# Whole-row gathers through DRAM in place of quarter-row gathers, in a routed mixture-of-experts kernel

## The chip, the cores and the metric

One core of a Trainium2 chip. The metric is device time in microseconds (us) for one execution of the whole program; lower is better. Five engines run their own instruction streams and meet at semaphores: TensorE (PE, matmul), VectorE (DVE), ScalarE (ACT), GpSimd (POOL) and SyncE (SP, which here only issues transfers). POOL issues the indirect DMAs (transfers whose row numbers come from a table in SBUF); SP issues the plain ones.

## The reference

A linear-attention layer `a` and a mixture-of-experts layer `b` read the same 2,048 tokens of 448 channels; a sigmoid gate mixes them. The expert part is what the change touches:

```
logits = xf @ w_gate                          # 8 experts
topk_idx = argsort(-logits)[:, :2]            # two experts for each token
gates = softmax(topk_val)
for e in range(8):
    h = silu(xf @ w1[e]) @ w2[e]              # 448 -> 1792 -> 448
    out = out + gate_of_e * h
out = g * a + (1 - g) * out
```

## The kernel before, in words

The first 230 us or so compute the attention layer and route the tokens. Routing writes, for each token and expert, a record (token number, weight) into a table in DRAM; the table is read back so that `idm` holds, for each expert, 4 columns of 128 token numbers, and `idx` the numbers of tokens over 512. Experts are handled in order of load: the code's expert 0 is the fullest. The room of an expert is fixed: 552, 544, 544, 504, 504, 504, 496 and 488 tokens (`ROOMS`, L31), so experts 0, 1 and 2 have a fifth, small chunk of 40, 32 and 32 tokens. The diff counts experts from 0; "experts 2 to 8" in the change's name are the code's 1 to 7.

An expert is 14 steps (`fc`, L1145), one for each 128 of its 1,792 hidden channels. A step has these parts:

- `load` (L726, transfers at L721): SP loads the weights of a pair of steps, 512 KB of `w1` and 448 KB of `w2`, into `wr` buffers. It is called one pair ahead of `halve`; the `w1` buffer exists twice, the `w2` buffer five times.
- `halve` (L733): ACT copies the weights into TensorE's float32r format, which keeps the high part (L739, `w1h`, `w2h`), and DVE subtracts to get the rest (L741, `w1l`, `w2l`). It is called for the pair after the current one.
- `first` (L943): TensorE computes `hp` for all tokens of the expert with 11 matmuls (L115), in one bank of PSUM for 504 tokens or fewer and in two halves for experts 0 to 2. There are two such banks. ACT applies silu (L961, `hs`), DVE makes the high and low parts `hx` (L967, L970).
- `second` (L988): one or two steps later TensorE multiplies `hx` by `w2` and adds into four or five PSUM accumulators `acc` (L1021, and L1004 for the small chunk).

At the end of an expert `leave` (L1032) scales the accumulators (L1038, L1040) and POOL adds the rows into the output in DRAM with indirect DMAs (L934).

The tokens of the next expert are brought in beside these steps. `gather` (L760) is called for chunk `c` at step 4 + `c`, `tokens` (L803) at step 9 + `c`. A token's row in DRAM is 512 floats: four quarters of 128. For expert 0 one indirect DMA fetches 128 whole rows (L768), a token in each partition. For the others the layout is another: partition 32a + i of a chunk holds, for b = 0 to 3, quarter a of token 32b + i. DVE's 32x32 transposes (L816) then give the layout with channels in partitions; ACT and DVE split it into the high and low parts `xgh` and `xgl` (L799, L800) that `first` multiplies. To fetch straight into that layout, four indirect DMAs, one for each b, fetch 128 quarter rows each (L772). Their indices `idq` are made by `quarters` (L921) in the first four steps of expert 0.

The `xg` buffers number five, so a chunk's gather waits until the chunk five before it is used up. The orders of PE, ACT and DVE are written out by hand. Those of POOL and SP are placed by a scheduler from the dependencies and a simulated time; each of the two queues runs its instructions strictly in the order so found.

Of the kernel before, what the change touches and what calls it, by code (L numbers as in the profile page):

```python
# [8 lines left out]
F32 = mybir.dt.float32  # L9
F32R = mybir.dt.float32r  # L10
BF16 = mybir.dt.bfloat16
I32 = mybir.dt.int32
AF = mybir.ActivationFunctionType
ALU = mybir.AluOpType
# [4 lines left out]
P = 128  # L19
# [5 lines left out]
E = 8  # L25
# [7 lines left out]
EX = EXS[0]  # L33
LARGE = len(EXS)
# [16 lines left out]
QASKS = {t: t + 7 for t in range(9)}  # L51
PEND = 0
ROWS = 1
SPLIT = 13
STORES = {3: 4, 4: 4, 5: 4, 6: 4}
VAHEAD = 6
# [18 lines left out]
def gated_mix(ctx: ExitStack, tc: tile.TileContext, xt, xq, wk, wq, wv, wphi, wo, w12, out):  # L75
    nc = tc.nc
    nm = MAIN // P

    cst = ctx.enter_context(tc.tile_pool(name="cst", bufs=1))
    dram = ctx.enter_context(tc.tile_pool(name="dram", bufs=1, space=DRAM))  # L80
# [8 lines left out]
    def after(i, others):  # L89
        for o in others:  # L90
            tc.add_manual_dep(i.ins, o.ins.name, mybir.DependencyInfo(mybir.DependencyClass.Sync,
                                                                      mybir.DependencyReason.DATA),
                              reason="what no_dep between its peers leaves out")

    def follow(i, o):
        tc.add_manual_dep(i.ins, o.ins.name, mybir.DependencyInfo(mybir.DependencyClass.NoSync,
                                                                  mybir.DependencyReason.SCHED_ONLY),
                          reason="what is needed sooner goes first")


    runs = {"on": False, "before": [], "last": [], "kind": None}

    def in_turn(i, kind=None):
        if runs["on"]:
            if kind is None or kind != runs["kind"]:
                runs.update(before=runs["last"], last=[], kind=kind)
            for o in runs["before"]:
                follow(i, o)
            runs["last"].append(i)
        return i  # L110

    def mm3(o, pairs):
        n = len(pairs)
        for i, (a, b) in enumerate(pairs):
            nc.tensor.matmul(o, a, b, start=i == 0, stop=i == n - 1)  # L115

    def split(hi, lo, src, hi_engine="act"):
        if hi_engine == "act":
# [31 lines left out]
    pe = pe_stack.enter_context(tc.tile_pool(name="pe", bufs=1, side="right"))  # L150
# [28 lines left out]
    start = ExitStack()  # L179
# [44 lines left out]
    tabx = cst.tile([P, LARGE, 2], F32, name="tabx")  # L224
    idm = cst.tile([P, E * nm], I32, name="idm")
    idx = cst.tile([EX, LARGE], I32, name="idx")
    idq = cst.tile([P, E, 4 * nm + 2], I32, name="idq")
    nc.gpsimd.memset(idq, 0)
    byrank = cst.tile([P, E], I32, name="byrank")
    nov_i = cst.tile([P, 1], I32, name="nov_i")  # L230
    etile = cst.tile([P, MAXOV], I32, name="etile")
# [7 lines left out]
    m = NSLOT // P  # L239
# [83 lines left out]
    for k, c in enumerate(FIRST):  # L323
# [4 lines left out]
        if k == 0:  # L328
            for i in range(2):
                nc.tensor.matmul(bank("A", f"warm{WARM + i}"), zero.bitcast(BF16)[:, 0:P], zero.bitcast(BF16)[:, 0:512],  # L330
                                 start=True, stop=True)
# [267 lines left out]
    routes = []  # L599
# [27 lines left out]
    def blocks(kvs):  # L627
        nc.scalar.activation(kvs[:, :, 0:56], kvp[:, 0:224].rearrange("p (g f) -> p g f", g=4), AF.Copy)
        yield
        kvt = bank("O", "kvt")  # L630
        for g in range(0, 4, 2):
            nc.tensor.transpose(kvt[:, g * 64:g * 64 + P], kvs[:, g:g + 2].rearrange("p g f -> p (g f)"), ident)
        kv = kvt[:, 0:256].rearrange("p (j d) -> p j d", j=NJ)[:, :, 0:DH + 1]
        nc.scalar.activation(B[:, :, 0:DH + 1], kv, AF.Copy, scale=hsign[:, 0:1])
        nc.vector.tensor_scalar(B[:, :, DH + 1:58], kv, hsign[:, 1:2], None, op0=ALU.mult)
# [4 lines left out]
    for t in range(NT):  # L640
# [17 lines left out]
        if 1 <= t < 5:  # L658
            fold("q", t - 1)
            c = t - 1  # L660
# [43 lines left out]
    b = blocks(kvs)  # L704
# [21 lines left out]
    def load(s):  # L726
        e, q = divmod(s, F // 256)
        if q == 0:
            whose[e] = nc.values_load(byrank[0:1, e:e + 1], engines=SPONLY, min_val=0, max_val=E - 1)
        raws[s] = stage(pm, whose[e], q, f"_{s}", 5)  # L730
# [12 lines left out]
    xg = {}  # L743
    x_rows = xq.rearrange("(s a) k -> s (a k)", a=4)

    def extra(e):
        return EXS[e] if e < LARGE else 0
# [9 lines left out]
        return 4 if narrow(e) else 2  # L757


    def gather(e, c):  # L760
        if c == nm and not extra(e):
            return
        n = 4 if c < nm else -(-extra(e) // 32)
        t = pm.tile([P, 4, P], F32, tag="xg", name=f"xg{e}{c}", bufs=nm + 1)
        xg[e, c] = t
        if e == 0:
            ids, m = (idm[:, e * nm + c:e * nm + c + 1], P) if c < nm else (idx[:, e:e + 1], EX)
            in_turn(nc.gpsimd.indirect_dma_start(out=t[0:m].rearrange("p a k -> p (a k)"), out_offset=None, in_=x_rows,  # L768
                                                 in_offset=bass.IndirectOffsetOnAxis(ap=ids, axis=0)))
            return  # L770
        for b in range(n):
            i = nc.gpsimd.indirect_dma_start(  # L772
                out=t[:, b], out_offset=None, in_=xq,
                in_offset=bass.IndirectOffsetOnAxis(ap=idq[:, e, 4 * c + b:4 * c + b + 1], axis=0))
            if e == 1:
                for o in runs["last"]:
                    follow(i, o)


    def low_parts(pool, t, name, eng=nc.vector):  # L780
        m, n = t.shape[0:2]
# [132 lines left out]
    def rows(lo, hi):  # L914
        in_turn(nc.gpsimd.tensor_scalar(idm[:, lo * nm:hi * nm], tabm.bitcast(I32)[:, lo * nm:hi * nm, 0], float(S - 1), None,
                                op0=ALU.min))
        if lo < LARGE:
            hi = min(hi, LARGE)
            in_turn(nc.gpsimd.tensor_scalar(idx[:, lo:hi], tabx.bitcast(I32)[0:EX, lo:hi, 0], float(S - 1), None, op0=ALU.min))

    def quarters():  # L921
        for a in range(4):
            qs = slice(32 * a, 32 * a + 32)
            for b in range(4):
                nc.vector.tensor_scalar(idq[qs, :, b:4 * nm:4],
                                        idm[32 * b:32 * b + 32].rearrange("p (e c) -> p e c", e=E),
                                        4.0, float(a), op0=ALU.mult, op1=ALU.add)
            nc.vector.tensor_scalar(idq[qs, 0:LARGE, 4 * nm], idx[0:32], 4.0, float(a), op0=ALU.mult, op1=ALU.add)
            nc.vector.tensor_scalar(idq[32 * a:32 * a + EX - 32, 0:LARGE, 4 * nm + 1], idx[32:EX],
                                    4.0, float(a), op0=ALU.mult, op1=ALU.add)  # L930
            yield

    def scatter_add(y, idx_ap):
        return nc.gpsimd.indirect_dma_start(  # L934
# [38 lines left out]
    def pieces(e):  # L973
        return 2 if extra(e) else 1
# [81 lines left out]
    def order(e):  # L1056
        return (*([nm] if extra(e) else []), *range(nm))
# [8 lines left out]
    def part_way():  # L1066
        for g in list(coming):
            if next(g, 0) == 0:
                coming.remove(g)

    at, k = None, 0
    for t in range(NT + 2):
# [28 lines left out]
        if t == PEND:  # L1101
            pe_stack.close()
            pm = ctx.enter_context(tc.tile_pool(name="pm", bufs=2, side="right", reuse_waits="tile"))
# [3 lines left out]
        if at is None and not routes:  # L1107
            routes.append(ranks())
            at = NT
        if at == NT and not stores and not routes:  # L1110
            table()
            at = t
        k = t - (NT if at is None else at)
        if k == ROWS:
            rows(0, 1)
        if k == ROWS + 3:
            rows(1, E)
        if ROWS <= k < ROWS + 3:
            for c in range(2 * (k - ROWS), min(2 * (k - ROWS) + 2, nm + 1)):
                gather(0, c)  # L1120
# [3 lines left out]
        part_way()  # L1124
        if ROWS + 2 <= k < ROWS + 3 + nm:
            g = first_tokens(k - ROWS - 2)
            next(g)
            coming.append(g)
        if SPLIT <= t < SPLIT + 3 and splits:
            if next(splits[0], 0) == 0:  # L1130
# [10 lines left out]
    pf = pf_stack.enter_context(tc.tile_pool(name="pf", bufs=2, reuse_waits="tile"))  # L1141
    load(1)
    held = []
    routes += [quarters(), overflow()]
    for s in range(E * NFC):  # L1145
        e, fc = divmod(s, NFC)
        k, i = divmod(s, 2)
        token = tokens(e + 1, fc - 9) if e + 1 < E and 9 <= fc <= 9 + nm else iter(())
        next(token, 0)
        if i == 0 and k + 2 < E * NFC // 2:  # L1150
            load(k + 2)
        if k + 1 < E * NFC // 2:
            for _ in halve(k + 1, 1 + i):
                pass
        next(token, 0)
        if e + 1 < E and 4 <= fc <= 4 + nm:
            gather(e + 1, fc - 4)
        for hf in range(pieces(e)):
            if (e, fc, hf) not in fill:
                first(e, fc, hf)  # L1160
        held.append((e, fc))
        advance(1)
        if e == E - 1 and fc > NFC - LATE:
            continue

        keep = 1 if e == 0 or fc == 0 or fc >= 7 else 2
        while len(held) > keep:
            h = held.pop(0)
            second(*h)
            if h[1] == NFC - 1:  # L1170
                leave(h[0], order(h[0]))
                if h[0] == E - 2:
                    settle()
# [11 lines left out]
    with tc.tile_pool(name="po", bufs=1) as po:  # L1185
        with tc.For_i(0, n_ov, 1) as it:
# [7 lines left out]
            ids = po.tile([P, 1], I32, name="ov_ids")  # L1194
# [5 lines left out]
                                         in_offset=bass.IndirectOffsetOnAxis(ap=ids[:, 0:1], axis=0))  # L1200
            both(xgh, xgl, by_pe(po, xo, P, "ov"))
            acc = bank("O", "ov_acc")
            for fc in range(NFC):
                q, i = divmod(fc, 2)
# [71 lines left out]
```

## Time and profile before

| | us |
|---|---|
| median of 3 runs (lowest, highest) | 833.13 (832.22, 835.84) |
| the profiled execution | 834.39 |
| its span, first to last instruction | 832.7 |
| PE busy / weight load (PEld) busy | 804.8 / 712.7 |
| DVE busy | 480.2 |
| ACT busy | 317.3 |
| POOL busy | 342.4 |

The profile is one execution. A row of the timeline has the start, the duration, the engine, the line of the kernel, the operation, and in brackets how long the engine had been idle and what ended that. A row of the waits has the engine and what it waited to start, then what it waited for, with the total in us, the number of times and the longest. A row of the windows has the start and end of a stretch, its length, then the busy time (and instructions) of PE, PEld, DVE, ACT and POOL, the clock that TensorE was granted (1.00 is full speed), the busy share of the DMA engines and GB/s.

### The profile page before, as it was taken

What the parts mean: (1) busy time and instruction counts of PE and PEld (TensorE: products, weight loads), DVE (VectorE), ACT (ScalarE), POOL (GpSimd) and SP (SyncE); (2) the same over time, 40 slices, a digit from 0 to 9 for tenths busy, and PEclk for the clock granted to TensorE, in tenths of its full rate; (3) what the DMA queues carried; (4) which work ended last, traced back from release to release, by engine and by line L of the source; (5) the groups of instructions that cost most, each with busy time, mean ns of one, the idle gap of its engine ahead of it and who ended that gap; (6) DMA issues with size and microseconds to landing.
All of it is one profiled execution on the core that took longest, in us unless ns stands there. A gap on an engine that the chain in (4) does not pass through costs nothing. (4 is left out here: it accounts for less than half of the span.)

```text
span 832.7 us, 14729 instructions
## 1 busy us (share of the span) xinstructions
PE 804.8 (97%) x5672; PEld 712.7 (86%) x5672; DVE 480.2 (58%) x1048; ACT 317.3 (38%) x553; POOL 342.4 (41%) x344
## 2 busy tenths in 40 slices
PE   9999999899999899999999999999989999999996
PEld 6988887778999789998999888888878888888885
DVE  4597976456775567456645554654555465375431
ACT  5543454345642334333333342342433334244221
POOL 6666876665406256026614350730531143003003
PEclk9999998999999899999999999999999999999999
DMA  8420000015143226423733362463345237225303
GB/s 231 134 81 2 1 3 24 24 39 172 56 164 136 67 88 170 129 73 125 168 90 122 117 148 98 140 148 107 112 125 133 99 125 185 95 94 134 101 1 44
DMA packets 38910, 85.45 MB, mean 103 GB/s; under 512 B 11216, under 2 KB 19552, under 8 KB 38836
## 3 DMA queue, kind: packets, MB, share of 16 engines
q1 hardware_dynamic: 28612, 67.85, 24.6%
q0 software_dynamic: 10224, 16.61, 10.3%
q8 instruction: 46, 0.75, 0.4%
q14 instruction: 28, 0.23, 0.1%
HBM read 71.62 MB, written 12.82 MB: 101 GB/s over the span
## 5 line engine op out<-in xcount | busy, mean ns | idle before, releaser
L1021 PE MATMUL acc<-w2h,hx 128*128 128x448 f32 (+3 forms) x910 | 278.5, 367 | 3.2 <-DVE hx L967 3.1
L772 POOL DMA_INDIRECT xg<-in_xq_dram,idq x114 | 120.6, 1058 | 224.5 <-ACT xgh L799 172.0
L115 PE MATMUL hp<-xgh,w1h 128*128 128x272 f32 (+4 forms) x616 | 198.0, 336 | 5.7 <-ACT hs L961 3.1
L961 ACT ACTIVATE hs<-hp 128x272 f32<-128x272 f32 (+4 forms) x154 | 74.1, 484 | 323.7 <-issue 204.1
L115 PE MATMUL hp<-xgh,w1l 128*128 128x272 f32 (+4 forms) x616 | 196.9, 335 | 0.0
L1021 PEld LDWEIGHTS acc<-w2h,hx 128*128 128x128 f32 (+3 forms) x910 | 169.2, 186 | 26.3 <-issue 5.3
L967 DVE CAST hx<-hs 128x504 fp32r<-128x504 f32 (+5 forms) x154 | 56.2, 365 | 222.9 <-ACT hs L961 194.6
L1021 PE MATMUL acc<-w2l,hx 128*128 128x448 f32 (+1 forms) x462 | 169.4, 367 | 0.0
L115 PEld LDWEIGHTS hp<-xgh,w1h 128*128 128x128 f32 x616 | 116.3, 189 | 17.2 <-ACT hs L961 3.7
L115 PEld LDWEIGHTS hp<-xgh,w1l 128*128 128x128 f32 x616 | 116.4, 189 | 9.7
L934 POOL DMA_INDIRECT out_dram<-y,tabm x32 | 53.5, 1670 | 160.0 <-ACT y L1038 98.3
L115 PE MATMUL hp<-xgl,w1h 128*128 128x272 f32 (+4 forms) x462 | 104.4, 334 | 0.7 <-issue 0.7
L1021 PEld LDWEIGHTS acc<-w2l,hx 128*128 128x128 f32 (+1 forms) x462 | 85.9, 186 | 8.5
L970 DVE TENSOR_TENSOR hx<-hs,hx 128x276 fp32r<-128x276 f32 (+5 forms) x168 | 85.1, 514 | 5.3
L115 PEld LDWEIGHTS hp<-xgl,w1h 128*128 128x128 f32 x462 | 77.0, 189 | 8.8 <-issue 0.7
L741 DVE TENSOR_TENSOR w1l<-wr,w1h 128x1024 fp32r<-128x1024 f32 x56 | 68.0, 1215 | 3.6 <-ACT w1h L739 2.6
L741 DVE TENSOR_TENSOR w2l<-wr,w2h 128x896 fp32r<-128x896 f32 x56 | 60.3, 1076 | 11.0 <-ACT w2h L739 7.7
L739 ACT ACTIVATE w1h<-wr 128x1024 fp32r<-128x1024 f32 x56 | 58.9, 1052 | 0.0
L739 ACT ACTIVATE w2h<-wr 128x896 fp32r<-128x896 f32 x56 | 52.9, 945 | 0.0
L799 ACT ACTIVATE xgh<-xgt 128x512 fp32r<-128x512 f32 (+5 forms) x35 | 20.9, 597 | 38.1 <-DVE xgt L816 28.8
L586 POOL TENSOR_TENSOR ek<-ek,sk 128x896 f32<-128x896 f32 x16 | 27.1, 1699 | 19.0 <-DVE sk L585 9.1
L455 POOL DMA_INDIRECT tabd<-rec,slot_i x32 | 31.5, 984 | 7.6 <-issue 7.3
(221 smaller groups left out, 1020.8 us busy)
## 6 DMA issues: line engine op xcount, KB each, us to landing
wr<-in_w_dram SPq DMA_DIRECT2D x56, 512.0 KB
wr<-in_w_dram SPq DMA_DIRECT2D x56, 448.0 KB
xr<-in_xt_dram SPq DMA_DIRECT2D x15, 256.0 KB
out_dram<-aos SPq DMA_DIRECT2D x16, 224.0 KB
xg<-in_xq_dram,idq POOLq DMA_INDIRECT x114
out_dram<-zero SPq DMA_DIRECT2D x5, 224.0 KB
wraw_v<-in_wv_dram SPq DMA_DIRECT2D x4, 229.0 KB
wraw_k<-in_wk_dram SPq DMA_DIRECT2D x4, 224.0 KB
```

The costliest lines, as they stand in the source:

```text
L115: nc.tensor.matmul(o, a, b, start=i == 0, stop=i == n - 1)
L455: i = in_turn(nc.gpsimd.indirect_dma_start(out=tabd[:, :], out_offset=bass.IndirectOffsetOnAxis(ap=at, axis=0), in_=what, in_offset=None), ...
L586: in_turn(nc.gpsimd.tensor_tensor(out=by_head(e), in0=by_head(e), in1=s_.unsqueeze(2).to_broadcast([P, 2 * H, DH]), op=ALU.mult))
L739: nc.scalar.activation(h, raws[s][layer - 1], AF.Copy)
L741: nc.vector.tensor_tensor(out=l, in0=raws[s][layer - 1], in1=h.bitcast(F32), op=ALU.subtract)
L772: i = nc.gpsimd.indirect_dma_start(out=t[:, b], out_offset=None, in_=xq, in_offset=bass.IndirectOffsetOnAxis(ap=idq[:, e, 4 * c + b:4 * c ...
L799: nc.scalar.activation(xh, src, AF.Copy)
L934: return nc.gpsimd.indirect_dma_start(out=out, out_offset=bass.IndirectOffsetOnAxis(ap=idx_ap, axis=0), in_=y, in_offset=None, compute_op= ...
L961: nc.scalar.activation(hs[:, tsl], hp[:, 0:n], AF.Silu)
L967: nc.vector.tensor_copy(h[:, tsl], hs[:, tsl])
L970: nc.vector.tensor_tensor(out=h[:, a + o:b + o], in0=hs[:, a:b], in1=h[:, a:b].bitcast(F32), op=ALU.subtract)
L1021: nc.tensor.matmul(acc[e][c][:m, 0:D], l, r, start=fc == 0 and k == 0, stop=fc == NFC - 1 and k == len(pr) - 1)
```

## The change

For experts 1 to 7 an indirect DMA now fetches 128 whole rows into a new tile `rows` (two buffers), a token in each partition; SP writes the tile to a piece of DRAM (`spare`) and reads it back with four plain DMAs, one for each quarter of the row, into the layout that `tokens` wants. The gather of chunk `c` is called at step 2 + `c`, the write at 3 + `c`, the read at 5 + `c`; `tokens` stays at 9 + `c`. The gather also waits for the last matmul that `mm3` has issued up to that point, which is the last `first` of the step before. The index table `idq`, its memset and `quarters` go.

```diff
+ASKED = 2
+FETCHED = 5
...
+    reached = {}
+
     def mm3(o, pairs):
         n = len(pairs)
         for i, (a, b) in enumerate(pairs):
-            nc.tensor.matmul(o, a, b, start=i == 0, stop=i == n - 1)
+            reached["pe"] = nc.tensor.matmul(o, a, b, start=i == 0, stop=i == n - 1)
...
-    idq = cst.tile([P, E, 4 * nm + 2], I32, name="idq")
-    nc.gpsimd.memset(idq, 0)
...
+    rows_of, spare = {}, {}
+
     def gather(e, c):
-        if c == nm and not extra(e):
+        ids, m = (idm[:, e * nm + c:e * nm + c + 1], P) if c < nm else (idx[0:extra(e), e:e + 1], extra(e))
+        at = bass.IndirectOffsetOnAxis(ap=ids, axis=0)
+        if e:
+            rows_of[e, c] = pm.tile([P, 512], F32, tag="rows", name=f"rows{e}{c}", bufs=2)
+            i = nc.gpsimd.indirect_dma_start(out=rows_of[e, c][0:m], out_offset=None, in_=x_rows, in_offset=at)
+            after(i, [reached["pe"]])
             return
+        t = pm.tile([P, 4, P], F32, tag="xg", name=f"xg{e}{c}", bufs=nm + 1)
+        xg[e, c] = t
+        in_turn(nc.gpsimd.indirect_dma_start(out=t[0:m].rearrange("p a k -> p (a k)"), out_offset=None, in_=x_rows,
+                                             in_offset=at))
+
+    def spill(e, c):
+        m = P if c < nm else extra(e)
+        spare[e, c] = dram.tile([m, 512], F32, name=f"spare{e}{c}")
+        nc.sync.dma_start(spare[e, c], rows_of[e, c][0:m])
+
+    def fetch(e, c):
         n = 4 if c < nm else -(-extra(e) // 32)
         t = pm.tile([P, 4, P], F32, tag="xg", name=f"xg{e}{c}", bufs=nm + 1)
         xg[e, c] = t
...
-        for b in range(n):
-            i = nc.gpsimd.indirect_dma_start(
-                out=t[:, b], out_offset=None, in_=xq,
-                in_offset=bass.IndirectOffsetOnAxis(ap=idq[:, e, 4 * c + b:4 * c + b + 1], axis=0))
-            if e == 1:
-                for o in runs["last"]:
-                    follow(i, o)
-
+        for a in range(4):
+            nc.sync.dma_start(t[32 * a:32 * a + 32, 0:n],
+                              spare[e, c][:, a * P:(a + 1) * P].rearrange("(b i) k -> i b k", i=32))
...
-    def quarters():
...
-    routes += [quarters(), overflow()]
+    routes.append(overflow())
...
-        if e + 1 < E and 4 <= fc <= 4 + nm:
-            gather(e + 1, fc - 4)
+        for c in range(nm + (extra(e + 1) > 0) if e + 1 < E else 0):
+            if fc == ASKED + c:
+                gather(e + 1, c)
+            if fc == ASKED + c + 1:
+                spill(e + 1, c)
+            if fc == FETCHED + c:
+                fetch(e + 1, c)
```

More of the change, by code (lines that the diff above doesn't have):

```diff
@@ L765, in gather @@
         xg[e, c] = t
[L766 to L770, printed above, removed]
-        for b in range(n):
-            i = nc.gpsimd.indirect_dma_start(
-                out=t[:, b], out_offset=None, in_=xq,
-                in_offset=bass.IndirectOffsetOnAxis(ap=idq[:, e, 4 * c + b:4 * c + b + 1], axis=0))
-            if e == 1:
-                for o in runs["last"]:
-                    follow(i, o)
+        for a in range(4):
+            nc.sync.dma_start(t[32 * a:32 * a + 32, 0:n],
+                              spare[e, c][:, a * P:(a + 1) * P].rearrange("(b i) k -> i b k", i=32))
     def low_parts(pool, t, name, eng=nc.vector):
@@ L919, in rows @@
             in_turn(nc.gpsimd.tensor_scalar(idx[:, lo:hi], tabx.bitcast(I32)[0:EX, lo:hi, 0], float(S - 1), None, op0=ALU.min))
-    def quarters():
[L922 to L931, printed above, removed]
     def scatter_add(y, idx_ap):
```

## The prediction

> **What bounds the kernel now.** I read the page first, then the expert stage by windows (the first expert from 230 us to about 310, the next two 80 us each, the following ones 70 to 75), then what TensorE waited for after 230 us.
>
> ```profile
> span 832.7 us, 14729 instructions
> ...
> PE 804.8 (97%) x5672; PEld 712.7 (86%) x5672; DVE 480.2 (58%) x1048; ACT 317.3 (38%) x553; POOL 342.4 (41%) x344
> ...
> L772 POOL DMA_INDIRECT xg<-in_xq_dram,idq x114 | 120.6, 1058 | 224.5 <-ACT xgh L799 172.0 <-issue 29.9 <-DVE idq L925 21.1
> ```
> ```profile
> 230.00:310.00 80.00, 75.70 (x463) 71.60 (x463) 48.66 (x151) 26.20 (x50) 31.65 (x31) 0.96 0.33 113
> 310.00:390.00 80.00, 78.95 (x516) 73.33 (x515) 49.26 (x129) 29.99 (x60) 30.34 (x26) 1.00 0.42 120
> 390.00:470.00 80.00, 78.95 (x526) 73.11 (x525) 46.23 (x115) 28.09 (x54) 36.64 (x30) 1.00 0.45 126
> 470.00:545.00 75.00, 75.00 (x356) 64.75 (x356) 40.84 (x74) 26.51 (x40) 31.25 (x25) 1.00 0.43 123
> 545.00:620.00 75.00, 71.83 (x333) 61.74 (x332) 38.67 (x70) 25.99 (x40) 23.12 (x20) 1.00 0.43 128
> 620.00:690.00 70.00, 70.00 (x327) 60.72 (x327) 38.46 (x70) 25.27 (x39) 19.07 (x17) 1.00 0.43 127
> 690.00:765.00 75.00, 75.00 (x353) 65.52 (x352) 42.05 (x76) 29.36 (x44) 11.92 (x8) 1.00 0.41 111
> ```
> ```profile
> PE hp L115 <- issue: 3.3, 2, 2.7
> PE acc L1021 <- DVE hx L967: 3.1, 1, 3.1
> PE hp L115 <- ACT hs L961: 3.1, 3, 1.0
> ```
>
> TensorE is the bound, and the matmuls of the expert stage are not touched. So the change can win only what TensorE loses: 4.30 us of idle time in the first window, 1.05 in each of the next two, 3.17 in the fifth, none in the others: 9.57 us together. The waits agree (9.5 us) and show that it is six gaps. The 114 gathers of POOL cost nothing by their 120.6 us. The question is whether they make the six gaps, so I looked at the two long ones in the timeline.
>
> ```profile
> 271.04 0.54 PE L115 MATMUL hp<-xgl,w1h 128*128 128x276 f32 x3
> ...
> 273.03 0.94 POOL L772 DMA_INDIRECT xg<-in_xq_dram,idq  x1 [0.30 <-issue]
> 273.81 0.40 ACT L961 ACTIVATE hs<-hp 128x276 f32<-128x276 f32 x1 [4.58 <-remote]
> ...
> 274.26 0.60 PE L115 MATMUL hp<-xgh,w1h 128*128 128x276 f32 x1 [2.68 <-issue]
> ...
> 277.35 0.62 PE L115 MATMUL hp<-xgl,w1h 128*128 128x276 f32 x2 [0.66 <-issue]
> ```
> ```profile
> 608.88 0.84 PE L115 MATMUL hp<-xgl,w1h 128*128 128x504 f32 x3
> 609.23 0.94 POOL L772 DMA_INDIRECT xg<-in_xq_dram,idq  x1 [0.30 <-issue]
> 611.76 0.59 ACT L961 ACTIVATE hs<-hp 128x504 f32<-128x504 f32 x1 [6.61 <-remote]
> ...
> 612.86 0.47 PE L1021 MATMUL acc<-w2h,hx 128*128 128x448 f32 x1 [3.13 <-DVE hx L967]
> ...
> 622.48 0.84 PE L115 MATMUL hp<-xgl,w1h 128*128 128x504 f32 x3
> ...
> 623.41 0.59 ACT L961 ACTIVATE hs<-hp 128x504 f32<-128x504 f32 x1 [0.36 <-PE hp L115]
> ```
>
> The reader is to see the delay between a finished `hp` and silu on it. At 623 us `hp` ends at 623.32 and ACT starts at 623.41, 0.09 us later, although POOL is adding output rows then. In the gaps `hp` ends at 271.58 and ACT starts at 273.81, 2.2 us later with nothing else to do; and 609.72 against 611.76, 2.0 us. TensorE then has no free `hp` bank (first gap) or no `hx` (second). Both times POOL is in, or has just ended, a run of quarter gathers one 0.30 us behind the other. The short gaps look the same, for instance:
>
> ```profile
> 303.54 0.40 ACT L961 ACTIVATE hs<-hp 128x276 f32<-128x276 f32 x1 [3.11 <-remote]
> 306.88 0.39 PE L115 MATMUL hp<-xgh,w1h 128*128 128x276 f32 x1 [0.96 <-ACT hs L961]
> ```
> ```profile
> ACT hs L961 <- remote: 27.4, 6, 6.6
> ```
> ```profile
> 675.37 0.95 POOL L772 DMA_INDIRECT xg<-in_xq_dram,idq  x1 [0.31 <-issue]
> 676.12 0.59 ACT L961 ACTIVATE hs<-hp 128x504 f32<-128x504 f32 x1 [4.68 <-remote]
> ```
>
> Silu is six times released by something the profile can't name, and at all six, from the one at 273.81 to the one at 676.12, POOL is in such a run or at its end. I take the runs of quarter gathers as the cause. What carries the delay, the trace doesn't show.
>
> The first gap has a second price, the clock:
>
> ```profile
> 274.26:280.38 6.12, 5.46 (x18) 5.02 (x19) 4.41 (x15) 2.53 (x4) 0.94 (x1) 0.50 0.07 21
> ```
>
> After it TensorE runs at clock 0.50; of 5.46 us busy half, 2.73, is lost.
>
> **The change, part by part.** *Gathers.* 114 quarter gathers go; 30 whole-row gathers come (five for each of two experts, four for each of five), a step apart, so the runs become single gathers. Their nearest rows, and what the other added work and waits are measured by:
>
> ```profile
> L768 POOL DMA_INDIRECT xg<-in_xq_dram,idm x4: 946/973/1098, 182.9 to 192.0; - x4
> ```
> ```profile
> L925 DVE TENSOR_SCALAR idq<-idm x16: 180/190/256, 240.5 to 252.5; 32x32 int32<-32x32 int32 x16
> ```
> ```profile
> L721 SPq DMA_DIRECT2D wr<-in_w_dram x112: 3/333/537, 189.5 to 781.7; - x112
> ```
> ```profile
> SPq L721 <- DVE w1l L741: 364.5, 45, 15.6
> ...
> POOL out_dram L934 <- DMA out_dram<-y,tabx: 14.2, 4, 4.5
> ```
> ```profile
> 483.99 0.90 SPq L721 DMA_DIRECT2D wr<-in_w_dram  x2
> ```
> ```profile
> 488.94 1.05 ACT L739 ACTIVATE w1h<-wr 128x1024 fp32r<-128x1024 f32 x1
> ...
> 498.85 1.05 ACT L739 ACTIVATE w1h<-wr 128x1024 fp32r<-128x1024 f32 x1
> ```
> ```profile
> 499.07 1.55 POOL L934 DMA_INDIRECT out_dram<-y,tabx  x1 [3.41 <-DMA out_dram<-y,tabx]
> ```
>
> A whole-row gather of 128 rows takes POOL 0.97 us, as long as a quarter gather: 30 x 0.97 = 29 us in place of 120.6, off the path either way. The gaps that go with the runs: 9.57 us of idle time and 2.73 us of slow clock, **12.30 us**. The bounds are 0, if the runs aren't the cause, and 12.30, since TensorE has no other idle time in those windows. I take the upper end: single gathers are nearer to the spaced adding of rows at 622 us, with its 0.09 us, than to the runs.
>
> *Index table.* `quarters` issues 24 DVE instructions of about 0.19 us (4.6 us); they lay in the first window, where DVE is busy 48.66 of 80 us. Nothing won. `overflow` moves four steps earlier, into the same free time, and its POOL instructions with it. If DVE had no room there, the 4.6 us would be won once; that isn't so.
>
> *The gather's new wait.* It stands on POOL until TensorE ends `first` of the step before. Behind it wait only later gathers and the adding of the expert's rows, which has a whole expert's time. Nothing.
>
> *Write and read back.* 30 writes and 30 x 4 = 120 reads on SP, which also issues the weights. A plain issue takes SP 0.33 us: 150 x 0.33 = 50 us, against 364.5 us in which SP merely waits for `w1` buffers. In one step at most a write and four reads: 1.7 us. The write stands on SP until its gather has landed, the read until the write has, and behind both are weight loads. How much may these be late? The pair issued at 483.99 is first used at 498.85: 14.9 us; two uses lie 9.91 us apart for two steps, so 5 us a step. The load of a pair waits for the pair two before to be split, about two steps ahead of its own place in the program; the write (called at 3 + c, gather released by the `first` of step 1 + c) waits about one step plus the landing. No row has the landing of such a gather; bounds are 0 and the longest wait of POOL for a DMA, 4.5 us, and I take 3, between. So a load is delayed by at most about 5 + 3 = 8 us of its 14.9; its landing has the rest. Cost 0 where POOL is prompt; where it isn't, see the third rival. The reads are called four steps, 20 us, before `tokens`; without that cover ACT's in-order queue would stall on `xg` for each chunk.
>
> *Traffic.* 28 x 256 KB + 2 x 64 KB = 7.5 MB are written and read again. At the 111 to 128 GB/s of the windows, with the DMA engines busy 0.33 to 0.45, that is 15 MB more over 460 us, 33 GB/s: room is there.
>
> Sum: 832.7 - 12.3 = 820.4 for the span. The profiled run took 834.39, 1.26 over the median of the runs shown; from that median, 833.13 - 12.3 = **820.8 us**.
>
> **The rivals.** *Only the first long gap goes.* The gaps after 300 us lie in the steps 9 to 13 where ACT and DVE also split tokens; if that work makes silu late, they stay, and only 2.68 + 0.66 + 2.73 = 6.1 us go: 827.0. For it: the first gap alone lies outside those steps. Against: at 611.76 ACT had been idle for 6.61 us.
>
> *The gathers don't do it.* The late starts are ACT's or TensorE's own, and coincide with the runs because these are frequent; gaps and clock stay: 833. For it: a run at 0.30 us spacing takes about 1.25 us a gather, so 114 of them fill some 143 of 460 us; against it: six of six by chance would be (143/460)^6, about 0.1%, though the bunching of work near `tokens` makes chance less unlikely than that. The Trainium skill, "SBUF — State Buffer", section "SBUF: two separate sides", gives a reason of this kind: only VectorE and GpSimd share a port, and TensorE and ScalarE never wait on anyone there; by that rule no gather could hold up silu, and the time would be 833. The late starts above, on ScalarE, speak against it as far as semaphores go, which the rule doesn't cover.
>
> *The write blocks the weights.* POOL is in order, and for the experts with a fifth chunk the adding of rows ends late: the last one starts at 499.07 and ends at 500.62, six steps into the expert. If the next gathers stand behind these, the first ends at 500.62 + 0.30 + 0.97 = 501.9, lands up to 4.5 us later, and the weight pair that now goes out at 483.99 goes out at 506.4 and misses its use at 498.85 by 7.5 us, and by about as much again for its own landing if that takes 4.5: 7.5 + 4.5 = 12 us. TensorE has a step, 5 us, in hand. Three experts have such a tail (the code's 0, 1, 2): 3 x 7 = 21 us against 12.3 won: 842. (The Trainium skill, "DMA: Bandwidth & Descriptors", section "Anatomy of one DMA — SWDGE (gpsimd) path", puts a transfer at about 2.0 us plus its bytes at 436 KB per us; an estimate by it for 256 KB is 2.6 us in place of each 4.5, a miss of 8.2 us, and 830 for this rival; no row here shows such a landing.) It decides where a weight pair goes out more than about 10 us later than now. For it: the tail; against: the scheduler places POOL's work by readiness, and the first gather is ready some 20 us before the tail ends.
>
> **How the numbers follow.** 0.5%, 4.2 us, is about what a measurement of this kernel can tell from no change. Chances: the forecast 0.50; only the first gap 0.17; gathers not the cause 0.20; the write blocks 0.13. Faster by over 0.5% (under 829.0): 0.50 and most of 0.17, 0.65; within: the 0.20, 0.20; slower: 0.13 and a little for new late starts beside the added transfers, 0.15. Low end: 820.8 less the 2.7 us by which the slowest run lay over the median, 818. High end: into the third rival, 838; about 0.07 lies above it and 0.06 below 818.
>
> **What would show it.** Right: PE idle under 1 us in each window from 230 to 765 us; clock 1.00 at 270 to 290; no silu released by "remote"; POOL gathers 30, several us apart; SP's weight issues within 8 us of their old place relative to use. Wrong: late silu in steps 2 to 9 beside gathers or reads (not runs but transfers are the cause); gaps kept at steps 9 to 13 (first rival); ACT waiting for `wr` to land (third rival).

## The result and the profile after

The changed kernel takes 821.18 us (median of 6; 819.70 to 822.79), the kernel before, beside it, 833.49 us (median of 6; 832.22 to 840.20): 12.3 us, or 1.5%, faster by the medians. The ratio, which is one of means, is 0.984, with a 95% interval of 0.980 to 0.987. The prediction said 820.8 us.

The kernel before, timed beside each experiment, took 833 to 835 us beside some (here called the first condition, to which the result above belongs) and 802.5 us beside others (the second), with nothing to tell beforehand which it would be, so numbers are compared only within one condition.

The page after:

```profile
span 818.0 us, 14811 instructions
...
PE 799.4 (98%) x5672; PEld 710.7 (87%) x5672; DVE 475.6 (58%) x1024; ACT 318.6 (39%) x553; POOL 254.5 (31%) x259
...
L769 POOL DMA_INDIRECT rows<-in_xq_dram,idm x28 | 30.5, 1090 | 58.3 <-DMA spare<-rows 28.5
```

The windows after, over the same stretches as in the prediction:

```profile
230.00:310.00 80.00, 80.00 (x512) 76.31 (x511) 51.69 (x147) 29.70 (x56) 5.27 (x7) 1.00 0.44 141
310.00:390.00 80.00, 80.00 (x532) 74.20 (x531) 47.08 (x120) 29.14 (x56) 15.91 (x11) 1.00 0.53 154
390.00:470.00 80.00, 80.00 (x515) 73.26 (x514) 45.52 (x111) 29.71 (x54) 21.07 (x14) 1.00 0.51 141
470.00:545.00 75.00, 75.00 (x350) 65.12 (x349) 43.17 (x75) 28.22 (x43) 21.59 (x16) 1.00 0.60 160
545.00:620.00 75.00, 75.00 (x350) 65.08 (x349) 39.83 (x71) 26.69 (x40) 12.58 (x10) 1.00 0.57 168
620.00:690.00 70.00, 70.00 (x329) 61.02 (x328) 37.51 (x68) 25.10 (x38) 11.23 (x8) 1.00 0.52 157
690.00:765.00 75.00, 75.00 (x356) 65.92 (x355) 40.30 (x73) 27.93 (x42) 8.16 (x6) 1.00 0.51 153
```

The length of the stretch and TensorE's busy time are equal in every row: TensorE has no idle time left in them, at clock 1.00. The 9.57 us of gaps and the half clock behind the first are gone. From the first silu to the last matmul the expert stage took 594.75 us (230.12 to 824.87) and takes 580.56 us (229.53 to 810.09): 14.2 us less, of which gaps and clock, as the prediction counts them, are 12.3. The other 1.9 us lie mostly in the gaps too: matmuls overlap, so a gap costs more than its idle time. Counted from the start of one matmul to the start of the next, against the usual distance in the changed kernel, the gaps cost 10.85 us in place of 9.57, the slow clock 2.8, and 0.5 is left. The first 230 us are untouched: PE is busy 219.52 us of them before and 219.37 after.

In the timeline after, silu follows `hp` at once, here beside work of POOL at the place of the second long gap:

```profile
606.24 1.64 POOL L932 DMA_INDIRECT out_dram<-y,tabm  x1 [48.68 <-ACT y L1036]
608.18 1.58 POOL L932 DMA_INDIRECT out_dram<-y,tabm  x1 [0.30 <-issue]
609.11 0.59 ACT L959 ACTIVATE hs<-hp 128x504 f32<-128x504 f32 x1 [0.36 <-PE hp L119]
610.06 1.57 POOL L932 DMA_INDIRECT out_dram<-y,tabm  x1 [0.30 <-DVE w2l L743]
611.62 0.59 ACT L959 ACTIVATE hs<-hp 128x504 f32<-128x504 f32 x1 [0.97 <-PE hp L119]
611.94 1.61 POOL L932 DMA_INDIRECT out_dram<-y,tabm  x1 [0.30 <-issue]
```

In the waits of ACT no silu is released by "remote" any more. I call a silu late if it starts over 0.45 us after both the end of its `hp` and ACT's previous operation. In the expert stage before, 14 are late, all beside quarter gathers or up to 2.4 us behind them; after, none.

The price is on SP's and POOL's queues, as their waits show:

```profile
SPq L723 <- DVE w1l L743: 249.5, 31, 11.9
SPq L780 <- DMA rows<-in_xq_dram,idm: 71.3, 20, 9.7
SPq L787 <- DMA spare<-rows: 36.1, 22, 4.3
```

SP now stands 71.3 us for gathers to land and 36.1 us for writes, and about as much less for `w1` buffers (249.5 us in place of 364.5). No wait of ACT or DVE for a transfer appears.

### The profile page after: what moved, and what is told of

Read it like the earlier page. It is cut to its first block, busy times and chain, and to the rows that moved or that the text cites. A ratio compares the mean times of both kernels' runs of the same rounds, so it can differ in the third digit from the quotient of the medians.

```text
span 818.0 us, 14811 instructions
## 1 busy us (share of the span) xinstructions
PE 799.4 (98%) x5672; PEld 710.7 (87%) x5672; DVE 475.6 (58%) x1024; ACT 318.6 (39%) x553; POOL 254.5 (31%) x259
## 5 line engine op out<-in xcount | busy, mean ns | idle before, releaser
L119 PEld LDWEIGHTS hp<-xgl,w1h 128*128 128x128 f32 x462 | 76.4, 188 | 8.0
L769 POOL DMA_INDIRECT rows<-in_xq_dram,idm x28 | 30.5, 1090 | 58.3 <-DMA spare<-rows 28.5
L932 POOL DMA_INDIRECT out_dram<-y,tabx x10 | 15.5, 1554 | 104.3 <-DVE y L1038 97.8
L457 POOL DMA_INDIRECT tabd<-rec,slot_i x32 | 31.5, 984 | 7.6 <-issue 7.2
```

Of the source, the lines that this page charges most:

```text
L119: reached["pe"] = nc.tensor.matmul(o, a, b, start=i == 0, stop=i == n - 1)
L457: i = in_turn(nc.gpsimd.indirect_dma_start(out=tabd[:, :], out_offset=bass.IndirectOffsetOnAxis(ap=at, axis=0), in_=what, in_offset=None), ...
L769: i = nc.gpsimd.indirect_dma_start(out=rows_of[e, c][0:m], out_offset=None, in_=x_rows, in_offset=at)
L932: return nc.gpsimd.indirect_dma_start(out=out, out_offset=bass.IndirectOffsetOnAxis(ap=idx_ap, axis=0), in_=y, in_offset=None, compute_op= ...
```

## The experiments

The theory: an unbroken run of quarter gathers on POOL makes silu late. Rivals: the place (token splitting in steps 9 to 13), the transfers and their bytes, the number of gathers, or any DMA that POOL issues.

**Apart by chunk, the old gathers (q_spaced).** The kernel before; each chunk's four gathers wait for the step they are called in (`reached` is as in the change).

```diff
-            if e == 1:
-                for o in runs["last"]:
-                    follow(i, o)
+            after(i, [reached["pe"]])
```

> The kernel before, its 114 quarter gathers kept, but those of a chunk held until the first of the step before has ended (chunk c at step 4 + c): groups of four, a step of 5 us or more apart, instead of runs of 8 to 17. Run theory (only long runs of gathers delay silu): no gap of TensorE in the expert stage, clock 1.00 after the routing, 820 to 823 us, as the changed kernel, without any write and read back. Rival, gathers as such (their number or their quarter rows delay silu wherever they stand): gaps come back in steps 4 to 8, 828 to 834. Rival, layout and DVE (what won was quarters going): 833.

Measured (first condition): 831.41 us, ratio 0.997 (0.995 to 0.999). Only some 3 us were won; the expectation failed. The reason is in the timeline. Four gathers take 4 x 1.25 = 5.0 us, a whole step, so with the first chunk held back by the adding of rows the groups join again; between the two lines of POOL stand 14 more gathers, 0.30 us apart. The late silu and TensorE's waits stay:

```profile
414.13 1.01 POOL L774 DMA_INDIRECT xg<-in_xq_dram,idq  x1 [0.30 <-issue]
...
433.54 0.94 POOL L774 DMA_INDIRECT xg<-in_xq_dram,idq  x1 [0.30 <-issue]
```
```profile
PE acc L1021 <- issue: 2.6, 5, 1.0
PE hp L117 <- issue: 2.4, 3, 1.1
```

So it didn't make the runs shorter, and says little on the theory.

**All in one run, away from the tokens (q_run_at_4).** The kernel before, its gathers waiting as in q_spaced; all gathers of the next expert are released at step 4.

```diff
-        if e + 1 < E and 4 <= fc <= 4 + nm:
-            gather(e + 1, fc - 4)
+        if e + 1 < E and fc == 4:
+            for c in range(nm + 1):
+                gather(e + 1, c)
```

> As the one with groups of four, but all 16 or 17 quarter gathers of an expert are released together at step 4: one run of some 20 us, outside the steps 9 to 13 in which ACT and DVE also split tokens. Run theory: silu starts 1.5 to 3 us late some time after the fourth gather of each run, as before; whether TensorE stands still depends on the step, so 822 to 834 with late silu in steps 5 to 8. Place rival (token work and not the run): no late silu, 820 to 823.

Measured (first condition): 858.21 us, ratio 1.031 (1.025 to 1.037). The gaps went with the run to steps where no tokens are split: all gaps of 1 us and more in the expert stage lie within a run or 2 us behind it. The place falls as the cause.

```profile
PE hp L117 <- issue: 16.8, 18, 1.7
```

**The changed kernel plus a run (plus_run).** Sixteen quarter gathers into a tile that nobody reads, at step 10 of each of the experts 0 to 6. The next four kernels alter only this addition.

```diff
+        if e + 1 < E and fc == 10:
+            for b in range(16):
+                after(nc.gpsimd.indirect_dma_start(
+                    out=junk[:, b], out_offset=None, in_=xq,
+                    in_offset=bass.IndirectOffsetOnAxis(ap=idm[:, e * nm + b % 4:e * nm + b % 4 + 1], axis=0)),
+                    [reached["pe"]])
```

> The changed kernel with 16 quarter gathers more for each expert but the last, released together at step 10, into a buffer that nobody reads: nobody waits for them, they only run. Run theory: late silu and gaps of 1 to 3 us return in most of the 7 runs, the clock drops where a gap is long; 826 to 838 us. Rival (the gathers matter only through what waits for them, their buffers or their order): no gap, 820 to 823.

Measured (first condition): 846.60 us, ratio 1.014 (1.010 to 1.019), 25 us over the changed kernel beside the same kernel before. The timeline of the second run, between its first and its last gather (14 more between them):

```profile
368.29 0.96 POOL L1164 DMA_INDIRECT junk<-in_xq_dram,idm  x1 [16.20 <-PE hp L119]
...
380.68 0.40 ACT L959 ACTIVATE hs<-hp 128x272 f32<-128x272 f32 x1 [4.36 <-remote]
...
388.00 0.94 POOL L1164 DMA_INDIRECT junk<-in_xq_dram,idm  x1 [0.30 <-issue]
...
388.49 0.40 ACT L959 ACTIVATE hs<-hp 128x272 f32<-128x272 f32 x1 [7.41 <-remote]
...
388.94 0.60 PE L119 MATMUL hp<-xgh,w1h 128*128 128x272 f32 x1 [6.17 <-ACT hs L959]
```

The reader is to see that ACT, idle for 7.41 us, starts silu only when the last gather is issued, and TensorE 0.05 us after that silu's end. In all seven runs no silu is late that starts within 5 us of the run's start, which is four gathers. And nearly the whole 25 us falls in the experts 0 to 2 (from first silu to first silu the experts 0, 1 and 2 take 85.8, 85.6 and 89.1 us, against 81.0, 76.4 and 77.9 in the changed kernel): there `hp` comes in two halves and silu is wanted twice a step; in the later experts only up to two silu of a run are late, and the `hp` bank that TensorE has in hand covers them, but for 0.3 us at 631.

**The same bytes without POOL (plus_sp).** The sixteen transfers are plain DMAs of SP, 64 KB each in pieces of 512 bytes.

```diff
+                after(nc.sync.dma_start(junk[:, b], xq[b * P:(b + 1) * P, :]), [reached["pe"]])
```

> The changed kernel with 16 plain DMAs more of 64 KB in pieces of 512 bytes for each expert but the last, issued by SP at step 10: the bytes and pieces of the run of 16 gathers, on the other queue. Run theory (POOL's indirect DMAs do it): no late silu, 820 to 824, at most a little for 16 x 0.33 = 5.3 us in which SP can't issue weights. Transfer rival (small pieces in dense order delay silu, whatever queue): late silu and gaps as with the added gathers, 826 to 838.

Measured (first condition): 820.48 us, ratio 0.983 (0.979 to 0.987), the changed kernel's own; TensorE's waits after 230 us are 0.02 us together. It is not the traffic as such.

**Four that told little (plus_run_small, plus_pool_plain, rows_run, plus_thin).** Sixteen gathers of 64 bytes a row in place of 512; sixteen plain DMAs issued by POOL; the changed kernel's own whole-row gathers all at step 2, with five buffers; the sixteen gathers two a step from step 6 on.

> As the changed kernel with the added run of 16 gathers at step 10, but each gathers 128 pieces of 64 bytes in place of 512: the same 16 instructions and 2,048 pieces, an eighth of the bytes. If instructions or pieces on POOL's queue hold up silu: late silu and TensorE gaps as with 512-byte pieces, about 840 to 850 us. If it is the bytes that go through that queue: few late starts, 820 to 826.

> As the changed kernel with the added run, but the 16 transfers that POOL issues are plain ones (128 rows of 512 bytes at fixed places) and not indirect. If any run of DMAs issued by POOL does it: 840 to 850 us with late silu. If it is the indirect form (an index read for each row): 820 to 824 and no late silu, as with the 16 plain DMAs on SP.

> The changed kernel with its own 30 gathers bunched: all four or five of an expert released together at step 2, five rows buffers in place of two; writes and reads where they were. If the length of a run counts (four or five make about 6 us): hardly a late silu, 820 to 823. If the bytes of a run count (as many as in a run of 16 quarter gathers): late silu and gaps in steps 2 to 5, 826 to 840.

> The changed kernel with the same 16 quarter gathers added for each expert but the last, two released at each of the steps 6 to 13 in place of all at step 10: POOL has half of each step free. If an unbroken run is needed: no late silu, no gap, 820 to 823 us. If each gather costs its share wherever it stands: about 846, as with the run.

All fell into the second condition (before: 802.55 us): 802.40, 802.27, 801.80 and 801.78 us, every ratio between 0.999 and 1.000, every interval within 0.998 to 1.002. They don't tell the rivals apart, but they tell something else. The run of sixteen was there, as long as ever (the first two rows are its first and last gather, from plus_run_small), and silu was prompt in it:

```profile
265.60 0.95 POOL L1164 DMA_INDIRECT junk<-in_xq_dram,idm  x1 [21.67 <-PE hp L119]
...
286.25 0.94 POOL L1164 DMA_INDIRECT junk<-in_xq_dram,idm  x1 [0.30 <-issue]
```
```profile
275.31 0.40 ACT L959 ACTIVATE hs<-hp 128x276 f32<-128x276 f32 x1 [1.29 <-PE hp L119]
276.64 0.40 ACT L959 ACTIVATE hs<-hp 128x276 f32<-128x276 f32 x1 [0.93 <-PE hp L119]
```

So the delay isn't a property of the program alone: in the second condition the runs cost nothing, and a kernel that is the changed one plus bunched gathers (rows_run) gains at most 0.15% over the kernel before. Two of the four were run again.

**Thin and small again (thin_again, small_again).**

> The kernel after the change, with 16 more quarter gathers that nothing reads in each of the experts 0 to 6, two at each of the token steps 6 to 13, so that no more than two follow each other. Read only if before takes about 833 us beside it. If it is the unbroken run that delays silu behind the end of hp: at most 3 us over the kernel after, so 820 to 824, ratio 0.985 to 0.989. If it is the number of gathers: as with 16 in one run at step 10, about 25 us more, so 840 to 850, ratio 1.01 to 1.02. If before takes about 802 us beside it, both give a ratio within 0.5% of 1.

> The kernel after the change, with 16 more gathers in one run at step 10 of each of the experts 0 to 6, each of 64 bytes per index in place of 512, which nothing reads. Read only if before takes about 833 us beside it. If it is the run of indirect DMAs on POOL that delays silu, whatever it moves: the run is as long as with 512 bytes, so about 25 us over the kernel after, 840 to 850, ratio 1.01 to 1.02. If it is the bytes that the gathers move: an eighth of the 25 us, 820 to 826, ratio 0.98 to 0.99. If before takes about 802 us beside it, both give a ratio within 0.5% of 1.

Measured (first condition): thin_again 820.25 us, ratio 0.981 (0.977 to 0.986); small_again 852.07 us, ratio 1.020 (1.016 to 1.025). An eighth of the bytes costs the full 25 us or more, so bytes fall; as many gathers, spread, cost nothing, so the number falls. What remains is the run. Thin_again also says how long it must be, since POOL, held for a buffer, let some of its pairs join. This is its longest run, seven gathers from 344.08 to 353.84:

```profile
344.08 1.77 POOL L769 DMA_INDIRECT rows<-in_xq_dram,idx  x1 [6.71 <-DMA spare<-rows]
346.15 0.96 POOL L1164 DMA_INDIRECT junk<-in_xq_dram,idm  x1 [0.30 <-issue]
...
352.90 0.94 POOL L1164 DMA_INDIRECT junk<-in_xq_dram,idm  x1 [0.30 <-issue]
```

One silu after it is late, by 0.87 us, another, at 420.02 behind three gathers, by 0.58 us, and TensorE doesn't stop. My expectation that no more than two would follow each other was wrong; that seven cost nothing here is the better knowledge.

**Whose side is late? (run_dve), and the form (pool_plain_again).** The first is plus_run with the edit below, which leaves out silu, the second the plain DMAs of POOL again.

```diff
-        nc.scalar.activation(hs[:, tsl], hp[:, 0:n], AF.Silu)
+        nc.vector.tensor_copy(hs[:, tsl], hp[:, 0:n])
```

> The kernel after the change with the 16 added quarter gathers in one run at step 10 of each of the experts 0 to 6, and the silu of hp left out: VectorE copies hp to hs in its place, so ScalarE has no part in that hand-off. Read only if before takes about 833 us beside it. If it is TensorE's signal that the run holds up: the copies start 2 to 10 us behind the end of hp within the runs, and the time is 835 to 855. If it is ScalarE that is held up: every copy starts within 1 us of the end of hp and no gap of TensorE lies in a run, 815 to 825. VectorE's own extra work (154 copies by some 0.45 us, 70 us on an engine with 344 us idle) may add a few us in both. If before takes about 802 us beside it, neither shows a late copy.

> The kernel after the change, with 16 plain DMAs of 128 x 512 bytes that nothing reads, issued by POOL in one run at step 10 of each of the experts 0 to 6. Read only if before takes about 833 us beside it. If it is a run of DMAs that POOL issues itself, indirect or not, that delays silu: the run has 16 x (0.57 + 0.3) = 14 us in place of 22, so some 12 to 18 us over the kernel after, 832 to 838, ratio 0.997 to 1.005. If it takes the indirect form (128 addresses each): 820 to 823, ratio 0.982 to 0.987. If before takes about 802 us beside it, both give a ratio within 0.5% of 1.

Both fell into the second condition (before: 802.48 us): 805.41 us, ratio 1.004 (1.002 to 1.005), and 802.16 us, ratio 1.000 (0.999 to 1.001). No copy in run_dve was late (none by over 0.04 us), as then expected of either theory. Both questions stay open as experiments.

**What the traces say to the first of them.** Plus_thin and thin_again are one kernel in the two conditions, and POOL issues indirect DMAs in its first 200 us too: the 32 scatters of the routing table (L457), in groups of up to four, 0.30 us apart. Thin_again has this wait of TensorE from 110 to 230 us (plus_thin has none of it):

```profile
PE n L869 <- issue: 8.9, 19, 1.2
```

Its timeline, TensorE and POOL, at one of these groups:

```profile
133.74 1.12 PE L869 MATMUL n<-B,et 64*64 64x60 f32 x48
133.95 1.00 POOL L457 DMA_INDIRECT tabd<-rec,slot_i  x1 [0.15 <-issue]
...
135.29 0.35 PE L869 MATMUL n<-B,et 64*64 64x60 f32 x4 [0.42 <-issue]
...
138.26 0.48 PE L869 MATMUL n<-B,et 64*64 64x60 f32 x3 [0.47 <-issue]
```

The same place in plus_thin:

```profile
133.58 1.19 PE L869 MATMUL n<-B,et 64*64 64x60 f32 x64
133.79 1.00 POOL L457 DMA_INDIRECT tabd<-rec,slot_i  x1 [0.15 <-issue]
```

In both, 64 short matmuls begin 0.21 us ahead of a group of three scatters. In the second condition they take 1.19 us. In the first TensorE does 48 of them, and the other 16 dribble on until 138.74, with waits for nothing that the profile shows: 5.0 us. Of its 16 such blocks eight take 1.8 us or more, and beside or just behind each of these POOL issues scatters or the gathers of expert 0; the other eight take 1.16. In plus_thin no block takes over 1.24 us. Every trace of the first condition has this wait (18 to 21 times, 8.1 to 9.7 us), every trace of the second has none. So under POOL's indirect DMAs TensorE itself is held up, ScalarE has no part in that. A long run does the same to the long matmuls, as here in q_run_at_4, at the end of a run that POOL issues until 455.92:

```profile
452.78 0.28 PE L117 MATMUL hp<-xgh,w1l 128*128 128x272 f32 x1
454.21 0.28 PE L117 MATMUL hp<-xgh,w1h 128*128 128x272 f32 x1 [1.15 <-issue]
...
455.63 0.29 PE L117 MATMUL hp<-xgh,w1h 128*128 128x272 f32 x1 [1.02 <-issue]
457.04 0.28 PE L117 MATMUL hp<-xgh,w1l 128*128 128x272 f32 x1 [1.12 <-issue]
458.47 0.84 PE L117 MATMUL hp<-xgl,w1h 128*128 128x272 f32 x3 [1.15 <-issue]
```

With the one left out these are the last eight of the eleven matmuls of one `hp`, and the three ahead of them already worked in the same bank, so neither silu nor a bank can be what they wait for.

That the late silu is the same thing, TensorE's side of the hand-off, is argued from this and not shown. The other hand-offs point the same way: in every trace of the first condition, runs included, all 154 copies of VectorE on `hs` start within 0.03 us, and ScalarE's 30 copies on VectorE's transposes within 0.04 us, of their input's end or the engine's previous operation. Of these hand-offs only the one from TensorE comes late. It is not the loading of instructions, at least in one run: in that of plus_run from 368.29 to 388.95 no packet of the instruction queues moves (the nearest start at 367.1, for 0.9 us, and 397.2).

## Why the prediction was right

*The mechanism.* The six gaps and the slow clock were put down to the runs, and all went, 12.30 us forecast, none left. Plus_run puts the delay back by runs alone; plus_sp, thin_again and small_again take away traffic, number and bytes. The Trainium skill, "SBUF — State Buffer", section "Who interferes with whom", says that TensorE and ScalarE never wait on anyone. Of SBUF's ports that may hold, and the second condition looks like it; in the first, runs on POOL made ScalarE wait 7.41 us at a time, and by that rule, taken for any wait, the change would have won nothing.

*The delay itself.* The prediction read it too small. It measures the two silu from an `hp` that they do not work on: TensorE has two banks, and by then both were full. Silu and `hp` taken in their order, the one at 273.81 works on the `hp` that ended at 267.34, and the one at 611.76 on the one that ended at 604.76; the `hp` that ended at 609.72 has its silu at 613.09, at once behind ACT's copy.

```profile
266.79 0.55 PE L115 MATMUL hp<-xgl,w1h 128*128 128x276 f32 x3
```
```profile
603.92 0.84 PE L115 MATMUL hp<-xgl,w1h 128*128 128x504 f32 x3
...
613.09 0.58 ACT L961 ACTIVATE hs<-hp 128x504 f32<-128x504 f32 x1
```

So ACT stood before a finished `hp` for all of the 4.58 and 6.61 us that its rows show, and not for 2.2 and 2.0. The sum does not suffer, since it goes by TensorE's gaps.

*Single gathers "a step apart".* Wrong as put. The gathers come in pairs 0.30 us apart, most often right behind the adding of rows: in the timeline above four additions stand behind each other, and two gathers follow at 613.86 and 615.59, 10.3 us of unbroken indirect DMAs without a late silu. The conclusion held; that it did because an addition comes only every 1.9 us, a gather every 1.25, and because two to four gathers are too few, fits all traces but was not tried apart.

*The landing.* Taken as 3 us, bounded by 4.5; mis-sized. For the code's expert 4, from a gather's end to its write it took 4.2 to 5.4 us: gathers ending at 478.46, 481.67, 487.59 and 490.69, writes at 483.75, 486.69, 491.76 and 496.07 (the second is an upper bound, since SP was issuing reads until 486.60). The prediction's smaller estimate, 2.6 us, was further off.

*SP's delay of the weights, at most 8 of 14.9 us.* Mis-sized; the cost of nothing held. The pair whose `w1` ACT first splits at 498.17 now goes out at 488.61, 9.6 us ahead; the corresponding pair had 17.3 us before (491.39 to 508.73), so it lost 7.8. But seven of the pairs lost more than 8 us, the worst 11.0 (570.61 to 590.61 before, 570.98 to 580.01 after), so that sign of being right did not come true. These seven had 19.8 us of lead or more, and the smallest lead left is 9.0 us. The pair that the prediction takes its 14.9 us from lost nothing (473.43 to 488.29).

```profile
488.61 0.76 SPq L723 DMA_DIRECT2D wr<-in_w_dram  x2
```
```profile
498.17 1.05 ACT L741 ACTIVATE w1h<-wr 128x1024 fp32r<-128x1024 f32 x1
```

*The other costs at nothing.* VectorE's 4.6 us of `quarters` are gone (480.2 to 475.6) and show nowhere in the time. POOL's busy time falls by 87.9 us, near the 120.6 - 29 forecast. The DMA engines' share rises in every window, to 0.60 at most, without a wait behind it.

*The rivals.* Only the first gap: false, q_run_at_4 has gaps where no token is split. The gathers don't do it: false in the first condition, and the very state of things in the second, which the prediction did not foresee as a condition. The changed kernel itself wasn't timed there, but rows_run and plus_thin, which add to it, equal the kernel before within 0.2%. The write blocks the weights: SP did wait up to 9.7 us for a gather, as that rival had it, but the lead of 9.0 us and more was enough, since the scheduler put the first gathers ahead of the last additions (477.45 and 480.46, with additions to 489.24).

The span fell by 14.7 us, the medians by 12.3. The profiled run before lies 0.9 us over its median, the one after 1.5 us under it; the better hit of the medians is partly luck.

## What to carry to other kernels

Look at what an engine off the critical path issues in bursts, not only at its busy time: POOL was 41% busy and still set all six of TensorE's gaps. If a hand-off is late with its engine idle and "remote" as the releaser, line it up against POOL's runs of indirect DMAs, and spread them; up to about four in a row, with several us to the next, cost the long matmuls nothing here. A short pause is not enough: in the kernel before eight gathers ended at 299.53, four more began at 300.53, and the silu at 303.54 was 3.1 us late. And time such a change in both conditions of the chip, for its whole gain can belong to one of them.

## What was not expected of the hardware

- A run of 16 indirect gathers, one each 1.25 us, delays silu by up to 8.1 us (10.2 in q_run_at_4), from about 5 us into the run on, whether a gather moves 64 KB or 8 KB. Runs of up to six additions into DRAM, one each 1.9 us, don't.
- The same kernel has this delay or not: thin_again and plus_thin take 820.25 and 801.78 us. The number of the chip doesn't tell which: it is 8 for plus_run, in the first condition, and for plus_thin, in the second. Their first silu starts at 230.08 and 212.12 us, and from there to the last matmul they take 580.56 and 580.57, so all of the difference lies ahead. The short matmul blocks place it: those at 133.74 and 133.58 are 0.2 us apart, those at 203.77 and 185.83 are 17.9 apart, and it stays so. Seven of the eight long blocks lie in that stretch, beside scatters and the gathers of expert 0, and take 14.1 us more than seven of 1.16; the rest isn't traced. Spreading the 32 scatters would be the next change to try; it wasn't run.
- The shortest matmuls feel even a single gather or two scatters (blocks of 2.3 and 2.1 us in place of 1.16); in the long ones of the experts TensorE stood still only with runs of eight or more.
- The clock fell to 0.50 from 273.55 to 280.38, with the first gap of the kernel before, 2.68 us, and not with the longer one of 3.13 us. The traces show why: the clock changes only on a grid of 3.413 us (in every trace its changes lie whole multiples of that apart). In the expert stages of all traces, a stretch of the grid at full clock in which TensorE stood idle 1.76 us or more was followed by 0.50, 11 times of 11, one with 1.56 us or less never; 1.71 us was, 1.74 was not. Of the first gap 1.97 us lay in one stretch, from 270.14; the longer gap was cut at 611.47 into 1.74 and 1.39.
- What holds TensorE up, and whether plain DMAs issued by POOL do it too, stays open.
